# Moving layer 2's first layer norm: 14 token tiles normalised and split in layer 1's spatial stage, ten of them stored and turned on loading

## The chip, the cores and the metric

One core of one Trainium2 chip runs the whole program as one launch. The metric is the device time of a launch in microseconds (us). The engines are named as in the profile: PE (TensorE, matmul), DVE (VectorE), ACT (ScalarE), POOL (GpSimd), SP (SyncE, which here issues the DMAs).

## The reference, cut to what matters

Two identical layers work on `x`, 2048 tokens by 640 features, float32. Each adds an attention with a compressive memory (32 heads of 20, four segments of 512 tokens), then a gMLP whose spatial product mixes all tokens:

```python
x = x + _A_ref(_layernorm(x, axis=-1), A_wq, A_wk, A_wv, A_wo, A_beta)
x = x + _B_ref(_layernorm(x, axis=-1), B_w_in, B_w_sp, B_b_sp, B_w_out)
x = x + _A_ref(_layernorm(x, axis=-1), A_wq, A_wk, A_wv, A_wo, A_beta)
x = x + _B_ref(_layernorm(x, axis=-1), B_w_in, B_w_sp, B_b_sp, B_w_out)
def _layernorm(x, axis=-1, eps=1e-5):
    m = jnp.mean(x, axis=axis, keepdims=True)
    v = jnp.var(x, axis=axis, keepdims=True)
    return (x - m) / jnp.sqrt(v + eps)
```

In `_B_ref` the spatial part is `g = einsum("ts,bsf->btf", w_sp, z2) + b_sp` and the output `einsum("bsf,fd->bsd", z1 * g, w_out)`. The change touches the third of these layer norms, the one ahead of layer 2's attention.

## The kernel before, in words

The tokens are cut into 16 tiles of 128; four tiles are one attention segment. Float32 values are carried through the matmuls as two float16 halves, high and low, and three products. A *split* makes these halves (ACT copies the high one, POOL or DVE subtracts for the low one), and a *turn* brings them from tokens-by-features into features-by-tokens with one transposing DMA issued by SP.

Each layer has three stages, which stand in the profiled execution at these times. Layer 1: attention (`phase1a`) to about 610 us, projections of the gMLP (`phase1b`) to 820, spatial stage (`phase2`) 820 to 1221. Layer 2: attention 1221 to 1760, `phase1b` to 1950, spatial stage (`phase2s`, another routine) to the end.

**Layer 1's spatial stage** goes over the 16 token tiles `t`. `product(t)` is the spatial matmul (L713). Behind it in program order stand the store of an earlier output tile, `split(t+1)` of the next weight rows, loads, `gate(t)` (ACT reads the product from PSUM at L724, DVE multiplies with `z1` at L726, and the result `u` is split and turned into `ut`), `scale(t+2)`, and `tail(t-1)`: the output matmul L745 and the addition L748, which makes the output tile `xo`. `xo` is stored to the DRAM tensor `x2_t`, layer 2's input. In iterations 6 to 9 this stage also runs `prep` of layer 2's tiles 0 to 3; in 10 to 13 it computes their values (`value`), and in 14 and 15 the first query and key units. There the orders of PE, SP, DVE and ACT are as written in the code (`manual_schedule`), POOL's is left to the scheduler.

**`prep(t)`** makes the attention input of token tile `t`: load `x2_t`; statistics on DVE (`bn_stats` twice L235, `bn_aggr` L236, `ve` L237); the power -1/2 on POOL (L238); the normalisation on DVE (L1074); split on ACT (L250) and POOL (L251); the turn (L252) into `self.xt[s % 2]`, the transposed input of segment `s = t // 4` (two buffers: `xt0` for even segments, `xt1` for odd). For tiles 4 to 15 `prep` is called in layer 2's attention.

**Attention** goes over pairs of heads. A pair's stack of queries, keys, masks and row maxima is a tile `qk`, filled by DMAs: `qk<-st` (L1272, from the DRAM tensor `st`, where `stack` stored the halves `qhl` and `khl` of a unit at L1261 and L1262) and `qk<-mr` (L1353, the row maxima). For each pair PE does the score products L1314 (`mp` for the maxima, which DVE reduces at L1330, then `es`, which ACT exponentiates into `P` at L1323) and the value products. Between the pairs PE runs denser work in the order of a list, which is for layer 2

```python
order = "02 03 v4 04 v5 v6 v7 10 11 12 13 14 v8 v9 v10 20 v11 21 p0 22 23 24 v12 v13 v14 30 v15 31 p1 32 33 p2 34 p3 ..."
```

with `20 v11 21` and `30 v15 31` changed to `v11 20 21` and `v15 30 31` and `33 p2` to `p2 33`. Two digits `sm` are unit `m` of segment `s` (its query and key projections, PSUM tiles `qps` and `kps`, L1152; `keys` then makes `phl` and turns it into `pk`, L1188), `vi` is the value projection of tile `i` (`vps`, L1095), and `pi` an output projection. `vi` reads the tile that `prep(i)` turned. In attention only PE's order is as written. A list scheduler sets the others: it takes instructions by priority on its own simulated clock, and `hold()` (`issue_after`) keeps `prep`'s instructions behind what was last issued when they were written. Each DMA of SP also waits for the one eight issues before it.

Of the kernel before, what the change touches and what calls it, by code (L numbers as in the profile page):

```python
# [9 lines left out]
F32 = mybir.dt.float32  # L10
F32R = mybir.dt.float32r
F16 = mybir.dt.float16
# [3 lines left out]
ALU = mybir.AluOpType  # L16
# [3 lines left out]
S, D, H, DH, NSEG = 2048, 640, 32, 20, 4  # L20
# [7 lines left out]
XS = 1024.0  # L28
# [197 lines left out]
def layernorm_stats(g, xt, d, nch, mult=1.0):  # L226

    nc = g.nc
    st = g.small.tile([128, nch, 6], F32, tag="lnst", name="lnst")
    mv = g.small.tile([128, 2], F32, tag="lnmv", name="lnmv")  # L230
    ve = g.small.tile([128, 1], F32, tag="lnve", name="lnve")
    rs = g.small.tile([128, 1], F32, tag="lnrs", name="lnrs")
    c = d // nch
    for i in range(nch):
        nc.vector.bn_stats(st[:, i, :], xt[:, i * c:(i + 1) * c])  # L235
    nc.vector.bn_aggr(mv, st)  # L236
    nc.vector.tensor_scalar(ve, mv[:, 1:2], EPS, mult ** -2, ALU.add, ALU.mult)  # L237
    nc.gpsimd.tensor_tensor(rs, ve, g.mhalf, ALU.pow)  # L238
    return mv, rs


def layernorm(g, xt, out, d, nch, mult=1.0):
    mv, rs = layernorm_stats(g, xt, d, nch, mult)
    return g.nc.vector.tensor_scalar(out, xt, mv[:, 0:1], rs, ALU.subtract, ALU.mult)


def split_t(g, hl, t, src, low=None):

    nc = g.nc
    nc.scalar.copy(hl[:, 0], src)  # L250
    (low or nc.vector).tensor_tensor(hl[:, 1], src, hl[:, 0], ALU.subtract)  # L251
    nc.sync.dma_start(t.rearrange("p i k c -> p (i k) c"), hl.rearrange("p i c -> p (i c)"), transpose=True)  # L252
# [404 lines left out]
def phase2(g, w_sp, x1_d, z1_d, zh, zl, out, nxt):  # L657

    nc, tc = g.nc, g.tc
# [3 lines left out]
    with ExitStack() as ctx:  # L663
# [6 lines left out]
        py = pool("cy", 1, space=PSUM)  # L670
        nxt.pd = pool("cpd", 2, space=PSUM)
        small = lambda nm: g.small.tile([128, 1], F32, tag=nm, name=nm)
        raw, ready, un = {}, {}, {}

        def rows(t):
            if t < NT:
                raw[t] = pr.tile([128, S], F32, tag="wr", name="wr")
                nc.sync.dma_start(raw[t], w_sp[t * 128:(t + 1) * 128, :])

        def scale(t):  # L680
            if t < NT:
                am, iv, un[t] = small("am"), small("wiv"), small("un")
                pw, ivw = g.wpw[:, t:t + 1], g.wiv[:, t:t + 1]
                nc.vector.tensor_reduce(am, raw[t], AX.X, ALU.max, apply_absolute_value=True)
                nc.vector.tensor_scalar(pw.bitcast(I32), am.bitcast(I32), 0x7F800000, None, ALU.bitwise_and)
                nc.vector.tensor_scalar(pw, pw, 2.0 ** -100, None, ALU.max)
                nc.vector.reciprocal(iv, pw)
                nc.vector.tensor_scalar(ivw, iv, WB, None, ALU.mult)
                nc.vector.tensor_scalar(un[t], pw, 1.0 / (WB * ZS), None, ALU.mult)

        def split(t, i):
            if t < NT:
                if i == 0:
                    ready[t] = (pt0, pt1)[t % 2].tile([128, 2, 2, NT // 2, 128], F16, tag=f"wt{t % 2}", name="wt")
                v = raw[t].rearrange("p (m i c) -> p i m c", i=2, c=128)[:, i]
                ivw = g.wiv[:, t:t + 1]
                p = i and t > 0
                hl = (ph1 if p else ph0).tile([128, 2, 1024], F16, tag=f"wn{int(p)}", name="wn")
                h, l = [hl[:, j].rearrange("p (m c) -> p m c", c=128) for j in range(2)]
                nc.scalar.activation(h, v, AF.Identity, scale=ivw)  # L700
                nc.vector.scalar_tensor_tensor(l, v, ivw, h, ALU.mult, ALU.subtract)
                nc.sync.dma_start(ready[t][:, i].rearrange("p l k c -> p (l k) c"), hl.rearrange("p l c -> p (l c)"), transpose=True)

        def store(t):
            for i in range(t % 2, 2):
                nc.sync.dma_start(g.turned[t][i], ready[t][:, i].rearrange("p l k c -> p (l k c)"))

        def product(t):
            gp = pg.tile([128, 2, 512], F32, tag="gp", name="gp")
            for i, k in enumerate(ks):  # L710
                for j, (a, b) in enumerate(((0, zh), (0, zl), (1, zh))):
                    for n in range(2):
                        nc.tensor.matmul(gp[:, n, :FHH], ready[t][:, k % 2, a, k // 2, :], b[:, k, n * FHH:(n + 1) * FHH],  # L713
                                         start=(i == 0 and j == 0), stop=(i == NT - 1 and j == 2))
            return gp

        def fetch(nm, src):
            o = p2.tile([128, src.shape[-1]], F32, tag=nm, name="c" + nm)
            nc.sync.dma_start(o, src)
            return o  # L720
# [19 lines left out]
        def tail(t, uh, ul, xs, x1):  # L740
            yp = py.tile([128, 2, 512], F32, tag="yp", name="cyp")
            for k in range(KO):
                for j, (a, b) in enumerate(((uh, woh), (uh, wol), (ul, woh))):
                    for n in range(2):
                        nc.tensor.matmul(yp[:, n, :320], a[:kn[k], k, :], b[:kn[k], k, n * 320:(n + 1) * 320],  # L745
                                         start=(k == 0 and j == 0), stop=(k == KO - 1 and j == 2))
            xo = px.tile([128, 2, 320], F32, tag="xo", name="xo")
            nc.vector.scalar_tensor_tensor(xo, yp[:, :, :320], xs, x1.rearrange("p (n c) -> p n c", n=2), ALU.mult, ALU.add)  # L748
            return lambda: nc.sync.dma_start(out[t], xo.rearrange("p n c -> p (n c)"))

        def behind(k):
            held = ExitStack()
# [22 lines left out]
        for t in range(NT):  # L775
            gp = product(t)
            sent()
            split(t + 1, 0)
            split(t + 1, 1)
            z1 = fetch("z1", z1_d[t])  # L780
            rows(t + 2)
            if t == 0:
                run(g.wu.load(sp, D, "wu", False))
            x1 = fetch("x1", x1_d[t])
            store(t)
            if t == 4:
                g.wu.keep()
            if 6 <= t < 10:
                parts = nxt.prep(t - 6)
            now = *gate(t, gp, z1), x1  # L790
            scale(t + 2)
            if 6 <= t < 10:
                for f in parts:
                    f()
            if pend is not None:
                sent = tail(*pend)
            pend = now
            if 10 <= t < 14:
                run(nxt.value(t - 10))
            if t >= 14:  # L800
                run(nxt.unit(0, t - 14))
        sent()
        tail(*pend)()


# [94 lines left out]
class Attention:  # L900
# [9 lines left out]
    def __init__(self, g, x, o_d, x1_d, kept):  # L910
        self.g, self.nc, self.tc = g, g.nc, g.tc
        self.x, self.o_d, self.x1_d = x, o_d, x1_d
        self.st = g.st
        self.u1, self.u2, self.vs, self.xt, self.mst = kept
        self.xt, self.vs = [self.xt, None], [self.vs, None]
        self.gm, self.ot = {}, {}
        self.phq = {}
        self.P, self.Pf, self.mx = {}, {}, {}
        self.pv, self.o = {}, {}
        self.wait, self.last, self.stacked = [], -1, -1  # L920
        self.held, self.readout = {}, set()
        self.now, self.later, self.rd = None, {}, set()
        self.last_of, self.marks = {}, {}

    def post(self, k, f, free=False):

# [53 lines left out]
    def head(self):  # L980
# [3 lines left out]
        with ExitStack() as ctx:  # L984
# [69 lines left out]
            for t in range(4):  # L1054
                for _ in self.value(t):
                    pass
                if t == 0:
                    with self.hold():
                        self.start()

    def prep(self, t, lead=False):

        g, nc = self.g, self.nc
        s, c = t // 4, slice((t % 4) * 128, (t % 4) * 128 + 128)
        xt = self.e2.tile([128, D], F32, tag="xt", name="xt")
        nc.sync.dma_start(xt, self.x[t])
        ln = []

        def stats():
            ln.extend(layernorm_stats(g, xt, D, 2, XS))  # L1070

        def norm():
            mv, rs = ln
            nc.vector.tensor_scalar(xt, xt, mv[:, 0:1], rs, ALU.subtract, ALU.mult)  # L1074
            hl = self.e1.tile([128, 2, D], F16, tag="xh", name="xnhl")
            split_t(g, hl, self.xt[s % 2][:, :, :, c], xt, low=nc.gpsimd)

        def held(f):
            with self.tc.high_priority(offset=HP) if lead else self.hold():
                f()  # L1080

        return lambda: held(stats), lambda: held(norm)
# [567 lines left out]
```

## Time and profile before

| | |
|---|---|
| runs | 2294.73, 2294.86, 2304.04 us (median 2294.86) |
| profiled execution | 2289.98 us, its span 2288.3 us |
| busy, share of the span | PE 94 %, DVE 66 %, ACT 51 %, POOL 43 % |
| mean granted TensorE clock | 0.987 |
| DMA | 350.41 MB, mean 153 GB/s |

The profiled execution lies 4.88 us below the median of the runs; 1.7 us of it lie outside the span. Rows give a line of the code (L1074), engine, operation, output`<-`input, and times in us (single instructions in ns where the row says "mean"). "Idle" is time in which an engine stood still ahead of an instruction, with what released it behind `<-`. PEclk is the granted TensorE clock as a share of the full one.

### The profile page before, as it was taken

To read this page: it belongs to the slowest core of one execution; us is meant where nothing else is said; L and a number is where in the kernel's file an instruction comes from. 1 tells how busy PE (TensorE), PEld (TensorE's weight loads), DVE (VectorE), ACT (ScalarE), POOL (GpSimd) and SP (SyncE) were. 2 spreads that over 40 slices of the span, in tenths; PEclk is the share of its full clock that TensorE was granted. 3 is DMA by queue.
4 is the path that set the end of the run, shared out by engine and by line. 5 is a ranking of instruction groups with operands and counts; after the bars stand their busy time and mean duration, and the time that the engine had idled before them with its cause. 6 is when DMAs were issued, how large, how long until landed. Compare 5 with 4: busy or idle time off the path is not lost.

```text
span 2288.3 us, 50426 instructions
## 1 busy us (share of the span) xinstructions
PE 2141.0 (94%) x20487; PEld 1285.7 (56%) x20487; DVE 1503.9 (66%) x2812; ACT 1174.3 (51%) x1464; POOL 975.1 (43%) x728
## 2 busy tenths in 40 slices
PE   4888899999799999999998888999998999999999
PEld 2555565656555555555554555656665555555655
DVE  7688878788755545354335788797776767556454
ACT  3389788788632332112112888887875334322221
POOL 2188788888610100000001889888885323000000
PEclk9999999999999999999999999999999999999999
DMA  5544634456655677878645336353466433977875
GB/s 161 154 109 122 156 84 125 117 146 144 170 133 141 176 199 198 253 196 215 177 122 140 77 109 165 96 124 103 123 170 174 110 104 100 264 215 188 227 211 128
DMA packets 512008, 350.41 MB, mean 153 GB/s; under 512 B 409952, under 2 KB 447712, under 8 KB 506656
## 3 DMA queue, kind: packets, MB, share of 16 engines
q1 hardware_dynamic: 511776, 347.19, 57.7%
q8 instruction: 160, 2.62, 0.5%
q14 instruction: 72, 0.59, 0.1%
HBM read 161.10 MB, written 97.93 MB: 113 GB/s over the span
## 4 chain that ended last, share of the span: by engine, by line
PE 69%; DVE 11%; ACT 7%; DMA 4%; issue 4%; POOL 4%; SPq 0%; ACTq 0%; DVEq 0%; POOLq 0%
PE zp L334 15%; PE gp L713 12%; PE cyp L745 4%; PE cyp L548 3%; PE pv L1367 3%; DVE mx L1330 3%; PE ga L499 3%; PE gb L499 3%; PE yps L1128 3%; PE vps L1095 3%; PE qps L1152 3%; ACT PH L1340 3%; PE mp L1314 2%; PE kps L1152 2%; POOL PL L1341 2%
## 5 line engine op out<-in xcount | busy, mean ns | idle before, releaser
L1341 POOL TENSOR_TENSOR PL<-P,PH 128x1280 f16<-128x1280 f32 x248 | 649.9, 2623 | 140.4 <-ACT PH L1340 135.8
L1330 DVE TENSOR_REDUCE mx<-mp 128x2 f32<-128x1024 f32 (+3 forms) x512 | 408.2, 818 | 93.9 <-PE mp L1286 92.5
L1323 ACT ACTIVATE P<-es,sc 128x1024 f32<-128x1024 f32 (+1 forms) x384 | 370.2, 964 | 118.2 <-PE es L1286 111.5
L1340 ACT CAST PH<-P 128x1280 f16<-128x1280 f32 x256 | 320.5, 1253 | 23.0 <-PE pv L1367 13.7
L238 POOL TENSOR_TENSOR lnrs<-lnve,mhalf 128x1 f32<-128x1 f32 x92 | 57.4, 632 | 579.6 <-DVE lnve L237 578.5
L334 PEld LDWEIGHTS <-th 128*128 128x128 f16 x1920 | 187.6, 98 | 164.6 <-DMA th<-xnhl 1.9
L713 PE MATMUL gp<-zh,wt 128*128 128x432 f16 x1024 | 231.2, 346 | 0.0
L713 PEld LDWEIGHTS <-wt 128*128 128x128 f16 x1536 | 150.2, 98 | 128.9
L1314 PEld LDWEIGHTS <-qk 60*128 60x128 f16 (+1 forms) x2048 | 93.5, 94 | 226.6 <-issue 167.3
L499 PEld LDWEIGHTS <-wt 128*128 128x128 f16 x1344 | 131.5, 98 | 112.6
L1314 PE MATMUL es<-qk 64*128 64x512 f16 (+3 forms) x1024 | 135.6, 300 | 44.5 <-ACT P L1323 35.5
L1367 PE MATMUL pv<-vs,PH 128*128 128x41 f16 x2560 | 168.6, 182 | 1.7 <-DVE ab L1383 1.4
L1367 PE MATMUL pv<-vs,PL 128*128 128x41 f16 x2560 | 163.8, 181 | 6.5 <-POOL PL L1341 6.0
L1314 PE MATMUL mp<-qk 60*128 60x512 f16 (+3 forms) x1024 | 138.2, 307 | 32.7 <-DVE mx L1330 31.7
L1095 PE MATMUL vps<-wvh,xt 128*128 128x320 f16 x640 | 151.9, 303 | 8.8 <-DVE vs L1101 6.6
L1367 PEld LDWEIGHTS <-PH 128*128 128x128 f16 x2560 | 142.6, 96 | 13.7 <-ACT PH L1340 1.7
L334 PE MATMUL zp<-wi1h,th 128*128 128x432 f16 x640 | 148.2, 346 | 2.0 <-DVE x L1134 1.3
L1367 PEld LDWEIGHTS <-PL 128*128 128x128 f16 x2560 | 142.8, 96 | 8.3 <-POOL PL L1341 7.3
L713 PE MATMUL gp<-zl,wt 128*128 128x432 f16 x512 | 135.3, 346 | 0.0
L1152 PE MATMUL kps<-xt,wkh 128*128 128x512 f16 x380 | 121.8, 388 | 8.7 <-DVE lnve L237 5.7
L726 DVE TENSOR_TENSOR u<-u,cz 128x864 f32<-128x864 f32 x16 | 17.0, 1060 | 165.7 <-ACT u L724 123.3
L1128 PE MATMUL yps<-woh,o 128*128 128x320 f16 x480 | 116.6, 306 | 1.4 <-DVE x L1134 1.4
(261 smaller groups left out, 4391.7 us busy)
## 6 DMA issues: line engine op xcount, KB each, us to landing
wr<-in_B_w_sp_dram SPq DMA_DIRECT2D x32, 1024.0 KB
qk<-st SPq DMA_DIRECT2D x256, 120.0 KB
x<-x SPq DMA_DIRECT2D x56, 320.0 KB
z<-z SPq DMA_DIRECT2D x32, 432.0 KB
cz<-z SPq DMA_DIRECT2D x32, 432.0 KB
turned<-wt SPq DMA_DIRECT2D x24, 512.0 KB
wt<-turned SPq DMA_DIRECT2D x24, 512.0 KB
st<-qhl SPq DMA_DIRECT2D x40, 256.0 KB
```

Of the source, the lines that this page charges most:

```text
L334: nc.tensor.matmul(zp[:, n, :FHH], a[:, k, :], b[:, k, c:c + FHH], start=(k == 0 and j == 0), stop=(k == KD - 1 and j == 2))
L499: nc.tensor.matmul(o[:, :FHH], wt[:, x, m, :], zb[b][:, y, m, :], start=start and i == j == 0, stop=i == NP - 1 and j == 2, skip_group_che ...
L713: nc.tensor.matmul(gp[:, n, :FHH], ready[t][:, k % 2, a, k // 2, :], b[:, k, n * FHH:(n + 1) * FHH], start=(i == 0 and j == 0), stop=(i == ...
L1095: nc.tensor.matmul(ps, a[:, k, c], b[:, k, n * 320:(n + 1) * 320], start=(i == 0), stop=(i == 14))
L1128: nc.tensor.matmul(ps, a[:, k, :], b[:, k, c], start=(i == 0), stop=(i == 14))
L1152: nc.tensor.matmul(ps, a[:, k, c], b[:, k, :], start=(i == 0), stop=(i == 14))
L1314: nc.tensor.matmul(out[:, h, o:o + w], a[r, ac], b[r, bc], start=o == 0, stop=False, skip_group_check=True)
L1323: self.last_of["ACT"] = nc.scalar.activation(P[:, :, 512 * c:512 * c + ew], es[:, :, :ew], AF.Exp, scale=g.esc).ins
L1330: self.last_of["DVE"] = nc.vector.tensor_reduce(self.mx[m][:, :, i], mp[:, :, o:o + w], AX.X, ALU.max).ins
L1340: nc.scalar.copy(PH, P[:, h])
L1341: (nc.gpsimd if h == 0 or n < self.N - self.TAIL else nc.vector).tensor_tensor(PL, P[:, h], PH, ALU.subtract)
L1367: nc.tensor.matmul(pv[:, i, h, :], x[:, c:c + 128], v[:, j, h0 + h, :], start=(j == 0 and x is PH), stop=(j == i and x is PL), skip_group_ ...
```

## The change

A new method `early(t, x)` does the normalisation and the split of layer 2's tile `t` from layer 1's output tile `xo`, which is still in SBUF, so that no load is needed. Iterations 2 to 15 of layer 1's spatial stage call it for tiles 0 to 13, ahead of `gate(t)`. Tiles 0 to 3 are turned at once into `xt[0]`, as before. For tiles 4 to 13 the two halves are stored as they are (320 KB) to a DRAM tensor `xn{t}`, and `prep(t)` in layer 2's attention becomes one transposing DMA from there (L1080). Tiles 14 and 15 keep the old `prep`. The `prep` calls of iterations 6 to 9 go.

```diff
@@ phase2
-        raw, ready, un = {}, {}, {}
+        raw, ready, un, made = {}, {}, {}, {}
...
             xo = px.tile([128, 2, 320], F32, tag="xo", name="xo")
+            made[t] = xo.rearrange("p n c -> p (n c)")
             nc.vector.scalar_tensor_tensor(xo, yp[:, :, :320], xs, x1.rearrange("p (n c) -> p n c", n=2), ALU.mult, ALU.add)
-            return lambda: nc.sync.dma_start(out[t], xo.rearrange("p n c -> p (n c)"))
+            return lambda: nc.sync.dma_start(out[t], made[t])
...
-            if 6 <= t < 10:
-                parts = nxt.prep(t - 6)
+            if t > 1:
+                nxt.early(t - 2, made.pop(t - 2))
             now = *gate(t, gp, z1), x1
             scale(t + 2)
-            if 6 <= t < 10:
-                for f in parts:
-                    f()
@@ Attention
+    def early(self, t, x):
+        g, nc = self.g, self.nc
+        xt = self.e2.tile([128, D], F32, tag="xt", name="xt")
+        layernorm(g, x, xt, D, 2, XS)
+        hl = self.e1.tile([128, 2, D], F16, tag="xh", name="xnhl")
+        if t < 4:
+            split_t(g, hl, self.xt[0][:, :, :, t * 128:(t + 1) * 128], xt, low=nc.gpsimd)
+            return
+        nc.scalar.copy(hl[:, 0], xt)
+        nc.gpsimd.tensor_tensor(hl[:, 1], xt, hl[:, 0], ALU.subtract)
+        self.normed[t] = nc.dram_tensor(f"xn{t}", (128, 2, D), F16, kind="Internal").ap()
+        nc.sync.dma_start(self.normed[t], hl)

     def prep(self, t, lead=False):
...
+        if t in self.normed:
+            o = self.xt[s % 2][:, :, :, c]
+            return lambda: None, lambda: nc.sync.dma_start(o.rearrange("p i k c -> p (i k) c"), self.normed[t].rearrange("p i c -> p (i c)"), transpose=True)
```

Line numbers of the kernel after are up to 16 higher than before from here on (L1152 becomes L1168, L1272 becomes L1288). The normalisation of the moved tiles stands at L244, in `layernorm`.

DVE, in an iteration of layer 1's spatial stage: `wn` is the low half of weight rows, `u` the gated product, `vs` values of an earlier tile. Before:

```order
L748 SCALAR_TENSOR_TENSOR xo<-cyp,xs,cx_15284 128x640
L1101 SCALAR_TENSOR_TENSOR vs<-vps,vs 128x16x20 x2
L701 SCALAR_TENSOR_TENSOR wn<-wr,wiv,wn 128x1024 x2
L726 TENSOR_TENSOR u<-u,cz_15723 128x864
L728 TENSOR_REDUCE uam<-u 128x1
```

The same place in the kernel after:

```order
L749 SCALAR_TENSOR_TENSOR xo<-cyp,xs,cx_15355 128x640
L1117 SCALAR_TENSOR_TENSOR vs<-vps,vs 128x16x20 x2
L701 SCALAR_TENSOR_TENSOR wn<-wr,wiv,wn 128x1024 x2
L235 BN_STATS lnst<-xo 128x6 x2
L236 BN_AGGR lnmv<-lnst 128x2
L237 TENSOR_SCALAR lnve<-lnmv 128x1
L244 TENSOR_SCALAR xt<-xo,lnmv,lnrs 128x640
L726 TENSOR_TENSOR u<-u,cz_15824 128x864
L728 TENSOR_REDUCE uam<-u 128x1
```

Five instructions of the norm now stand ahead of the gate's multiplication; 14 iterations have them.

SP, where layer 2's attention begins: `xnhl` are a tile's two halves, `x2_14` and `x2_15` layer 1's last output tiles. Before:

```order
L749 DMA x2_14<-xo_16226 128x640
L1272 DMA qk4_16389<-st0 60x1024
L1272 DMA qk5_16396<-st0 60x1024 x2
L252 DMA_TRANSPOSE xt1_16392<-xnhl_16466 128x10x128
L749 DMA x2_15<-xo_16323 128x640
L1261 DMA st0<-qhl_16475 128x512
L1262 DMA st0<-qhl_16475 128x2x512
L1066 DMA xt_16564<-x2_6 128x640
L1261 DMA st0<-khl_16502 128x512
L252 DMA_TRANSPOSE xt1_16392<-xnhl_16471 128x10x128
L1262 DMA st0<-khl_16502 128x2x512
```

After:

```order
L750 DMA x2_14<-xo_16372 128x640
L1288 DMA qk4_16535<-st0 60x1024
L1288 DMA qk5_16542<-st0 60x1024 x2
L750 DMA x2_15<-xo_16469 128x640
L1080 DMA_TRANSPOSE xt1_16538<-xn4 128x10x128
L1080 DMA_TRANSPOSE xt1_16538<-xn5 128x10x128
L1277 DMA st0<-qhl_16591 128x512
L1278 DMA st0<-qhl_16591 128x2x512
L1277 DMA st0<-khl_16618 128x512
L1278 DMA st0<-khl_16618 128x2x512
L1080 DMA_TRANSPOSE xt1_16538<-xn6 128x10x128
L1080 DMA_TRANSPOSE xt1_16538<-xn7 128x10x128
```

Two turns instead of one stand ahead of the store of `qhl`, and the turns of tiles 6 and 7 directly behind that of `khl`.

SP some 30 us later, among the fetches of the first pairs (`pk` are turned keys, `mr` row maxima). Before:

```order
L1188 DMA_TRANSPOSE pk_16608<-phl_16605 128x8x128
L1261 DMA st0<-khl_16760 128x512
L1353 DMA qk1_16386<-mr_16771 2x4x128
L1262 DMA st0<-khl_16760 128x2x512
L1353 DMA qk1_16386<-mr_16771 2x4x128
L1066 DMA xt_16828<-x2_7 128x640
L1272 DMA qk0_16385<-st0 60x1024 x2
L1188 DMA_TRANSPOSE pk_16817<-phl_16814 128x8x128
L1353 DMA qk2_16387<-mr_16890 2x4x128 x2
```

After:

```order
L1204 DMA_TRANSPOSE pk_16722<-phl_16719 128x8x128
L1080 DMA_TRANSPOSE xt0_174<-xn8 128x10x128
L1277 DMA st0<-khl_16861 128x512
L1080 DMA_TRANSPOSE xt0_174<-xn9 128x10x128
L1278 DMA st0<-khl_16861 128x2x512
L1369 DMA qk1_16532<-mr_16872 2x4x128 x2
L1080 DMA_TRANSPOSE xt0_174<-xn10 128x10x128
L1288 DMA qk0_16531<-st0 60x1024
L1204 DMA_TRANSPOSE pk_16918<-phl_16915 128x8x128
L1288 DMA qk0_16531<-st0 60x1024
L1080 DMA_TRANSPOSE xt0_174<-xn11 128x10x128
L1369 DMA qk2_16533<-mr_16989 2x4x128 x2
```

The turns of tiles 8 to 11, which segment 2 reads, now stand here, long before their values; their buffer `xt0` is free once unit 04 has been computed. The turns of tiles 12 and 13 stand behind unit 14 (about 1400 us in the execution before).

More of the change, by code (lines that the diff above doesn't have):

```diff
@@ L923, in __init__ @@
         self.last_of, self.marks = {}, {}
+        self.normed = {}
     def post(self, k, f, free=False):
```

## The prediction

> **What bounds the kernel now.** I read the page first, then busy time in stretches of layer 1's spatial stage and layer 2's attention, then what PE waits for in that attention, then groups and the timeline at the waits that the change touches. The page:
>
> ```profile
> span 2288.3 us, 50426 instructions
> PE 2141.0 (94%) x20487; PEld 1285.7 (56%) x20487; DVE 1503.9 (66%) x2812; ACT 1174.3 (51%) x1464; POOL 975.1 (43%) x728
> PE 69%; DVE 11%; ACT 7%; DMA 4%; issue 4%; POOL 4%; SPq 0%; ACTq 0%; DVEq 0%; POOLq 0%
> ```
>
> PE is the bound: busy 94 %, and 69 % of the chain that ended last. The change leaves PE's work and its order as they are, so it can only win idle time of PE, 147.3 us in all, or clock.
>
> Busy time by stretch (columns after the length: busy us and instructions of each engine, granted clock, DMA share, GB/s):
>
> ```profile
> core 0: us, PE busy (x) PEld busy (x) DVE busy (x) ACT busy (x) POOL busy (x), PEclk, DMA share, GB/s
> 820.00:1221.00 401.00, 401.00 (x2389) 233.41 (x2388) 177.90 (x311) 84.62 (x93) 13.82 (x17) 1.00 0.72 193
> 1221.00:1760.00 539.00, 491.54 (x6884) 311.44 (x6883) 410.13 (x801) 413.55 (x521) 429.60 (x291) 0.98 0.48 125
> 1221.00:1241.00 20.00, 14.25 (x65) 5.76 (x64) 7.92 (x14) 5.75 (x9) 5.42 (x5) 0.84 0.70 170
> 1261.00:1281.00 20.00, 16.16 (x249) 11.36 (x243) 15.94 (x31) 15.40 (x19) 12.68 (x7) 1.00 0.30 75
> 1371.00:1431.00 60.00, 53.31 (x777) 35.56 (x778) 51.21 (x107) 48.72 (x64) 54.60 (x40) 1.00 0.59 160
> 1431.00:1501.00 70.00, 67.78 (x983) 42.92 (x980) 55.21 (x109) 58.27 (x75) 60.24 (x42) 1.00 0.33 90
> 1501.00:1541.00 40.00, 36.73 (x490) 22.61 (x487) 37.37 (x74) 31.88 (x42) 33.83 (x26) 0.91 0.56 145
> 1541.00:1571.00 30.00, 26.22 (x385) 18.61 (x382) 21.65 (x45) 22.54 (x31) 27.61 (x22) 0.97 0.48 101
> ```
>
> Layer 1's spatial stage, which receives the norms, is PE without a gap, with DVE busy 44 %, ACT 21 % and POOL 3 %. Layer 2's attention, which loses them, leaves PE idle for 47.5 us while DVE, ACT and POOL are each busy for over 75 %. So the work goes from where the other engines are short to where they have room. The stretches with the norms of tiles 4 and 5 (1221 to 1241), 7 (1261 to 1281), 8 to 11 (1371 to 1431) and 12 and 13 (1501 to 1541) have PE idle for 29, 19, 11 and 8 %; the stretch 1431 to 1501, which has no norm, for 3.2 %. The excess over 3.2 % is 3.2 us in the second, 4.8 in the third and 2.0 in the fourth. That is the pool of the gain; 1541 to 1571 (tiles 14 and 15) has an excess of 2.8.
>
> **What the change removes from the attention.** By form, 1221 to 1760:
>
> ```profile
> L251 POOL TENSOR_TENSOR xnhl<-xt,xnhl 128x640 f16<-128x640 f32 x12 | 17.2, 1434 | 10.0 <-ACT xnhl L250 8.5 <-PE es L1286 1.4
> L1074 DVE TENSOR_SCALAR xt<-xt,lnmv,lnrs 128x640 f32<-128x640 f32 x10 | 14.7, 1471 | 0.0
> ...
> L235 DVE BATCH_NORM_STATS2 lnst<-xt 128x6 f32<-128x320 f32 x20 | 8.8, 482 | 0.6 <-DMA xt<-x 0.5
> L250 ACT CAST xnhl<-xt 128x640 f16<-128x640 f32 x12 | 8.6, 720 | 12.3 <-DMA xt<-xnhl 6.2 <-PE cyp L745 3.1 <-DVE xt L1074 1.7
> L238 POOL TENSOR_TENSOR lnrs<-lnve,mhalf 128x1 f32<-128x1 f32 x12 | 6.6, 551 | 7.8 <-DVE lnve L237 7.8
> ```
>
> For ten tiles (tiles 4 and 5 were already normalised, in part, before 1221): POOL 10 x (1.43 + 0.55) = 20 us, DVE about 8 x (2 x 0.48 + 1.47) = 19 us, ACT 10 x 0.72 = 7 us, and ten loads of 320 KB; the ten turns stay. None of this is on PE, so it counts only where PE waits.
>
> **What it adds in layer 1's spatial stage: nothing.** Groups of 820 to 1221:
>
> ```profile
> L724 ACT ACTIVATE u<-gp,bsp,un 128x864 f32<-128x864 f32 x16 | 17.1, 1069 | 161.7 <-PE gp L713 161.7
> ...
> L1074 DVE TENSOR_SCALAR xt<-xt,lnmv,lnrs 128x640 f32<-128x640 f32 x6 | 3.7, 613 | 3.4 <-POOL lnrs L238 3.3
> ```
>
> The new rows stand ahead of the gate. Per tile DVE gets 2 x 0.48 of statistics, some 0.3 for two small rows, 0.57 of waiting for POOL's power (3.4 / 6) and 0.61 of normalisation: 2.5 us. ACT gets 0.72, POOL 0.55 + 1.43. ACT stands still for 161.7 / 16 = 10.1 us per tile until PE ends the product, and the new work fits in that time, since `xo` is made an iteration earlier. On SP the new store waits for POOL's subtraction, and what queues behind it is the gate's turn `ut`, which comes later still. Ten stores of 320 KB (0.33 MB) less four loads are 2 MB on the 77 MB of the stage (193 GB/s for 401 us), 2.5 % on a DMA share of 0.72. If the cover were gone, 14 x 2.5 = 35 us would be on the path. Ends 0 (PE has no gap there to win) and a loss of 35; I take 0, since a delay must exceed 10 us to reach PE.
>
> **Start of the attention, 1221 to 1241 (tiles 4 and 5).** Timeline (start, duration), then two rows of the chain for the landing times:
>
> ```profile
> 1224.75 0.89 DVE L748 SCALAR_TENSOR_TENSOR xo<-cyp,xs,cx 128x640 f32<-128x640 f32 x1 [5.79 <-DMA x<-xo]
> ...
> 1225.70 1.36 SPq L252 DMA_TRANSPOSE xt<-xnhl  x1
> ...
> 1227.10 0.70 SPq L749 DMA_DIRECT2D x<-xo  x1
> 1227.91 0.38 SPq L1261 DMA_DIRECT2D st<-qhl  x1
> 1228.38 0.41 SPq L1262 DMA_DIRECT2D st<-qhl  x1
> ...
> 1229.15 0.72 ACT L250 CAST xnhl<-xt 128x640 f16<-128x640 f32 x1 [5.52 <-DMA xt<-xnhl]
> ...
> 1233.90 0.69 ACT L1185 ACTIVATE phl<-kps,sc 128x512 f16<-128x512 f32 x1 [2.94 <-DVE kps L1176]
> ...
> 1234.97 0.70 DVE L1186 SCALAR_TENSOR_TENSOR phl<-kps,sc,phl 128x512 f16<-128x512 f32 x1
> ...
> 1235.72 1.01 PE L1152 MATMUL kps<-xt,wkh 128*128 128x512 f16 x2 [5.66 <-DVE lnve L237]
> ```
>
> ```profile
> 1215.97 2.16 DMA st<-khl
> ...
> 1225.70 3.38 DMA xt<-xnhl
> ```
>
> PE waits 5.66 us for the PSUM tile that `phl` reads last; the row names `lnve`, but `phl` (L1186) ends at 1235.67. ACT's copy for tile 5 waited 5.52 us for a turn and held up everything behind it on ACT. That goes. What is late next is the halves' buffer: `phl` takes the one of `qhl`, so `qhl` must have been stored. By the order SP now issues `x2_15` (ready at 1225.6), two turns and then `qhl`: 1225.7 + 0.70 + 2 x 1.36 + 0.79 and two gaps of some 0.08 is 1230.1. With a landing of 2.16 to 3.38 and 0.69 + 0.70 for `phl`, PE goes on between 1233.7 and 1234.9: a gain of 0.8 to 2.0. I take 1.5. Upper end: the whole wait, and with it the halved clock behind it (7 x (1 - 0.53) = 3.3, next rows), 9.0. Lower end: two turns instead of one ahead of `qhl`, nothing else won: -1.4.
>
> **The ramp, 1261 to 1281 (tile 7; turns of 8 to 11 now amid the fetches).** Tile 7's normalisation leaves DVE (1.47). Two turns now stand ahead of the `qk<-mr` of a pair; at 1.36 each, half of it on the path is 1.4. I take 0. Ends: the whole excess, +3.2, and four turns' issue in full on the path, -5.4.
>
> **1371 to 1431 (tiles 8 to 11).** A row of ACT's timeline, and two of the tile views for the turn from DRAM (`o`, median, mean and longest ns) beside those from SBUF:
>
> ```profile
> 1417.19 0.59 ACT L1394 CAST ohl<-oat 128x480 f16<-128x480 f32 x1 [2.00 <-DMA xt<-xnhl]
> ```
>
> ```profile
> L1110 SPq DMA_TRANSPOSE o<-o x24: 1327/1372/2324, 330.9 to 1742.9; - x24
> ```
>
> ACT's output split waits 2.00 us behind a copy that needs the buffer of a turn. Copies, subtractions and turns of these four tiles leave the stretch; the turns have long landed. Excess 4.8 us, less half a turn (0.7) for those of tiles 12 and 13, which now stand near it on SP: 4.1. Ends: the two turns in full on the path and nothing won, -2.7, and 4.8. A turn from DRAM costs SP 1.37 us, as from SBUF, so I count no more for it.
>
> **1501 to 1541 (tiles 12 and 13).** The clock by stretches of PE, and the two waits of PE's timeline ahead of the slow part:
>
> ```profile
> core 0: us, PE busy (x), PEclk, DMA share, GB/s
> 1528.00:1536.00 8.00, 7.02 (x64) 0.57 0.49 145
> 1235.00:1242.00 7.00, 6.28 (x22) 0.53 0.32 86
> ```
>
> ```profile
> 1526.05 0.28 PE L1314 MATMUL es<-qk 64*128 64x256 f16 x2 [0.61 <-ACT P L1323]
> ...
> 1528.98 0.61 PE L1314 MATMUL mp<-qk 60*128 60x512 f16 x2 [1.55 <-DVE mx L1330]
> ```
>
> DVE's normalisation stands ahead of the maxima for which PE waits, and after these two waits, 2.2 us in 3.5, the granted clock is 0.57 over 8 us: 3.4 us of lost work. With the norms gone I expect the waits to go (the excess, 2.0) and the drop with them, since they stand right ahead of it: 5.4. Ends 0 (nothing is added there) and 5.4.
>
> [...]
>
> **1541 to 1571 (tiles 14 and 15 keep `prep`):** 0, since their work is unchanged. Ends 0 and 2.8, its excess.
>
> **Sum:** 1.5 + 0 + 4.1 + 5.4 = 11.0 us. Against the profiled execution (span 2288.3, 2289.98 with what lies around it) that is 2279.0; it ran 4.9 us under the median of 2294.86, from which I get 2283.9. A change of 0.5 %, 11.5 us, is about what a measurement can tell from none.
>
> **Rivals.** (1) The start clears too. If ACT's copy was the true cause and `qhl` is stored in time, the wait of 5.66 and its clock drop go (9.0 in place of 1.5), and a lighter POOL queue takes the excess of tiles 14 and 15 (2.8): 21.3 us, 2273.6. For it: ACT's 5.52 us. Against: two turns now ahead of `qhl`.
> What PE waits for most at the scores in the attention (us in all, times, longest):
>
> ```profile
> PE es L1314 <- ACT P L1323: 13.2, 20, 1.4
> PE mp L1314 <- DVE mx L1330: 9.9, 17, 1.5
> PE es L1314 <- DMA qk<-mr: 7.7, 4, 4.1
> ```
>
> (2) The waits refill. These are short and on ACT, DVE and DMA in turn, so that the next dependency may close a gap, and a drop of the clock may come at another place. Only the start and half of 1371 to 1431 stay: 1.5 + 2.0 = 3.5 us, 2291.4. That DVE is busy for 51 of 60 us there speaks for it.
> (3) Slower: the turns in the way. Eight turns of 320 KB (tiles 4 to 11) now stand at the start and in the ramp among `st` and `mr` transfers. PE's longest wait for an `mr` transfer was 4.1. If each holds the chain for its landing time, 3.38 us, 8 x 3.38 = 27.0 us are lost and 11.0 won: 2310.9. It decides from 11.0 + 11.5 = 22.5 us, 2.8 per turn. Against it: SP's own part is 1.36, the DMA share there is 0.30, and PE has other work between the pairs.
> (4) The drop stays. If the clock near 1528 falls for another cause than the two waits ahead of it, its 3.4 us are not won: 11.0 - 3.4 = 7.6, 2287.3. For it: waits of over 1 us stand at other places without a drop, since PEclk is 1.00 in 1371 to 1431, where PE is idle for 11 %. Against it: the two here are close together. [...]
>
> **How the numbers follow.** Forecast (a gain of 8 to 17 us, 2278 to 2287): 0.44. Rival 1: 0.17. Rival 2: 0.19. Rival 3: 0.08. Rival 4: 0.10. The late gate in the spatial stage: 0.02, at 2330. Faster by over 0.5 %: rival 1 and that part of the forecast with a gain over 11.5, 0.28, together 0.45. Slower: most of rival 3 and the late gate, 0.09. Same: the rest, 0.46. The range leaves out rival 3, the late gate (0.10) and the part of rival 1 under 2270 (0.05); its upper end lies 5.6 us over rival 2, about the lower end of the ramp's term: 2270 to 2297.
>
> **What would show it.** Right: only two sets of L235 to L238 (tiles 14 and 15) in the attention, PE idle under 3 us in 1371 to 1431, clock near 1.00 at 1528, the first wait for `kps` about 4 us and still with a clock of half behind it, layer 1's spatial stage still at 401 us with PE full. Wrong: longer `qk<-mr` waits of PE or a spread between score products from 1255 to 1285 (rival 3); `es` and `mp` waiting as long as before, 23 us over the attention, with other names (rival 2); PE gaps at L745 in the spatial stage (late gate).

## The result, and the profile after

The changed kernel took 2274.74 us (median of 4, 2271.51 to 2278.71) against 2294.80 before: ratio 0.992, 95 % interval 0.9896 to 0.9944. Run a second time on another occasion ("again" below) it gave 0.993 (0.9915 to 0.9946). So it is faster by 0.7 to 0.8 %, 17 to 20 us. The profiled execution took 2271.51 us. Its page, and its stretches of the spatial stage, of the attention and of the places that the prediction named:

```profile
span 2269.1 us, 50425 instructions
PE 2135.3 (94%) x20487; PEld 1282.5 (57%) x20487; DVE 1501.6 (66%) x2812; ACT 1175.6 (52%) x1464; POOL 976.3 (43%) x728
```

```profile
core 0: us, PE busy (x) PEld busy (x) DVE busy (x) ACT busy (x) POOL busy (x), PEclk, DMA share, GB/s
817.00:1218.00 401.00, 401.00 (x2389) 233.46 (x2388) 191.76 (x351) 92.33 (x104) 32.04 (x35) 1.00 0.74 197
1218.00:1740.00 522.00, 484.98 (x6881) 308.89 (x6880) 394.32 (x761) 406.89 (x511) 412.52 (x273) 0.99 0.49 123
1218.00:1238.00 20.00, 15.84 (x81) 7.10 (x80) 7.98 (x11) 4.90 (x8) 0.69 (x1) 0.91 0.80 187
1363.70:1418.60 54.90, 52.71 (x776) 35.22 (x778) 43.53 (x85) 45.73 (x60) 46.56 (x32) 1.00 0.54 132
1488.50:1523.20 34.70, 33.69 (x491) 21.41 (x487) 32.17 (x64) 31.20 (x41) 30.08 (x22) 1.00 0.51 138
1523.00:1555.00 32.00, 28.91 (x419) 20.53 (x416) 24.12 (x49) 23.37 (x31) 28.00 (x22) 0.95 0.39 90
```

The spatial stage still takes 401 us with PE full, although DVE, ACT and POOL have 14, 8 and 18 us more to do there. The attention is 17 us shorter, and PE's idle time in it falls from 47.5 to 37.0 us. What PE waits for there:

```profile
PE es L1330 <- ACT P L1339: 10.0, 14, 1.4
PE mp L1330 <- DVE mx L1346: 8.2, 17, 2.8
PE es L1330 <- DMA qk<-mr: 7.2, 4, 4.0
PE kps L1168 <- DVE phl L1202: 4.2, 2, 3.8
```

PE runs the same matmuls in the same order in all kernels of this study. So a stretch can be measured from one of its instructions to another, wherever it lies in time. The table gives lengths of such stretches (us). The row "before" and the last column give the lengths themselves, all other fields the difference to the profile before. The stretches are named by their times in that profile. B is the sum of 1248 to 1276 and 1276 to 1290; the columns left out (1290 to 1371, 1431 to 1501, 1576 to 1661) change by 0.31 or less.

| kernel | A 1221-1248 | B 1248-1290 | C 1371-1431 | D 1501-1541 | E 1541-1576 | 1661-1760 | attention |
|---|---|---|---|---|---|---|---|
| before | 26.96 | 42.22 | 59.70 | 39.99 | 35.00 | 99.12 | 539.07 |
| after | -2.78 | -1.60 | -4.82 | -5.31 | -1.09 | -1.02 | 522.46 |
| again | -4.25 | -1.61 | -4.80 | -5.30 | -1.02 | +0.94 | 523.08 |
| keep1213 | -2.76 | -1.47 | -4.98 | +0.78 | -1.31 | +0.05 | 529.38 |
| keep811 | -2.41 | -1.63 | +2.96 | -5.31 | +0.11 | +2.31 | 535.10 |
| keep47 | +0.43 | -0.17 | -4.68 | -5.31 | -2.27 | +1.29 | 528.42 |
| stores | +0.19 | -0.33 | +0.80 | +2.42 | +0.03 | +0.28 | 542.79 |
| dveback | +0.36 | -0.23 | -0.85 | -4.42 | -2.36 | +0.98 | 532.65 |
| splitback | -2.92 | -0.22 | -4.32 | -4.52 | -2.14 | +0.60 | 525.81 |
| jit | -2.10 | -1.63 | -4.49 | -5.32 | -0.95 | +0.82 | 525.53 |
| behind | -2.52 | -1.65 | -4.82 | -5.32 | -0.99 | -1.19 | 522.65 |
| spread47 | -6.17 | -0.21 | -4.82 | -5.30 | -1.10 | +0.84 | 522.51 |
| all16 | -1.94 | +0.58 | -0.07 | -5.30 | -5.41 | -1.11 | 525.94 |
| chain1213 | -2.52 | -1.55 | -4.84 | -1.90 | -0.82 | -1.60 | 525.75 |

Of the gain of 16.6 us (16.0 in "again"), A, B, C and D make 14.5 (16.0) and E 1.1 (1.0). The last 1.0 stands in 1661 to 1760; in "again" that stretch is 0.9 longer than before, so this is no steady gain. Beyond the attention the times of single executions spread without the change: PE's work up to 610 us, at which none of the edits is aimed, took 603.4 us in this execution and 606.6 in that of before, and 603.4 to 615.0 over all 14.

### The profile page after: what moved, and what is told of

It reads as the page before. It is cut to its first block, busy times and chain, and to the rows that moved or that the text cites. A ratio compares the mean times of both kernels' runs of the same rounds, so it can differ in the third digit from the quotient of the medians.

```text
span 2269.1 us, 50425 instructions
## 1 busy us (share of the span) xinstructions
PE 2135.3 (94%) x20487; PEld 1282.5 (57%) x20487; DVE 1501.6 (66%) x2812; ACT 1175.6 (52%) x1464; POOL 976.3 (43%) x728
## 5 line engine op out<-in xcount | busy, mean ns | idle before, releaser
L1168 PE MATMUL kps<-xt,wkh 128*128 128x512 f16 x380 | 120.7, 385 | 6.3 <-DVE phl L1202 6.3
L1168 PE MATMUL qps<-xt,wqh 128*128 128x512 f16 x380 | 116.9, 379 | 1.6 <-DMA xt<-xnhl 1.2
```

The costliest lines, as they stand in the source:

```text
L1168: nc.tensor.matmul(ps, a[:, k, c], b[:, k, :], start=(i == 0), stop=(i == 14))
```

## The experiments

**Which tiles pay where.** Three kernels leave one group of tiles with the old `prep`.

```diff
-            if t > 1:
+            if t > 1 and t - 2 < 12:                 # keep1213
+            if t > 1 and not 8 <= t - 2 < 12:        # keep811
+            if t > 1 and not 4 <= t - 2 < 8:         # keep47
                 nxt.early(t - 2, made.pop(t - 2))
```

> Tiles 12 and 13 keep the old preparation in layer 2's attention; tiles 0 to 11 are moved as in the kernel after. The attention (PE's work from 1221 to 1760 in the profile before) took 539.1 us before and 522.5 after. Local theory (each stretch's gain belongs to the norms that stood in it): PE's work of 1501 to 1541 loses its 5.3 us again, clock drop included, all other stretches stay as after within 0.5 us, attention 527.8 us. Rival, spread theory (less load on all engines and a new order from the scheduler win everywhere a little): two tenths of 16.6, 3.3 us, not bound to that stretch, attention 525.8 us.

Measured: 2287.02 us, ratio 0.9959 (0.9944 to 0.9974). D is back at 40.77, all other stretches up to E stay within 0.3 us of after.

> Tiles 8 to 11 keep the old preparation; all else as in the kernel after. Local theory: PE's work of 1371 to 1431 loses its 4.8 us again, the other stretches stay within 0.5 us, attention 527.3 us. Spread theory: four tenths of 16.6, 6.6 us over several stretches, attention 529.1 us. If the four early turns of tiles 8 to 11 had cost anything in 1248 to 1290, that stretch would get faster than after, by up to 5 us.

Measured: 2285.59 us, ratio 0.9950 (0.9935 to 0.9965). C is back, and 3 us beyond before; A, B and D stay. B did not get faster without the four early turns. Of the 12.6 us that the attention lost, 7.8 are C; 1.2 are E and 3.3 are 1661 to 1760, where the clock is halved for 3.4 and 6.8 us longer than in the kernel after.

> Tiles 4 to 7 keep the old preparation; all else as in the kernel after. Local theory: PE's work of 1221 to 1290 loses its 4.4 us again (2.8 at the start, 1.6 in the ramp), later stretches stay within 0.5 us, attention 526.9 us. Spread theory: 6.6 us over the whole attention, 529.1 us.

Measured: 2282.98 us, ratio 0.9942 (0.9925 to 0.9958). A and B are back, C and D stay; E is 1.2 shorter than after, without its drop of the clock (3.4 us). Most of each loss lies where its tiles' norms stood, and the spread theory falls. Sizes are less regular: the three losses (6.9, 12.6 and 6.0) sum to 25.5, more than the 16.6 won. C of keep811 and D of keep1213 each hold a clock drop of 3.4 us:

```profile
1366.90:1429.50 62.60, 54.80 (x776) 36.03 (x778) 51.25 (x105) 48.42 (x64) 54.57 (x40) 0.97 0.63 163
```

```profile
1496.40:1537.10 40.70, 35.76 (x488) 22.40 (x484) 37.95 (x75) 31.70 (x42) 35.12 (x26) 0.96 0.56 149
```

**What the added part costs.** Early norms and stores stay, but the attention prepares tiles 4 to 15 as before.

```diff
-        if t in self.normed:
+        if t in ():
```

> Everything that the change adds in layer 1's spatial stage is kept (14 early norms, ten stores), but tiles 4 to 15 are prepared in the attention as before, so the ten stored tiles are not used. Local theory: the additions cost nothing, so spatial stage 401 us, attention 539 us, time as before, 2294.8 within 4 us. Rival (the additions cost something that the gain hid): slower than before by that cost; 14 tiles at 2.5 us would be 35 us.

Measured: 2297.56 us, ratio 1.0007 (0.9996 to 1.0018). Its spatial stage:

```profile
822.10:1223.10 401.00, 401.00 (x2389) 233.49 (x2388) 194.90 (x361) 92.38 (x103) 33.35 (x37) 1.00 0.74 198
```

So the 14 early norms cost nothing where they stand. In the kernel after, ACT still waits 115.4 us for PE's products there (161.7 before):

```profile
L724 ACT ACTIVATE u<-gp,bsp,un 128x864 f32<-128x864 f32 x16 | 17.1, 1070 | 115.4 <-PE gp L713 115.4
```

The attention of "stores" took 3.7 us more than before, 2.4 of it in D; why stays open.

**Which part of the preparation was the cost.** dveback brings back the load and DVE's part (with POOL's power), splitback the load, ACT's copy and POOL's subtraction, chain1213 all of it in its chain for tiles 12 and 13; each into a tile that nothing reads, with the turn still from DRAM.

```diff
         if t in self.normed:
+            xt = self.e2.tile([128, D], F32, tag="xt", name="xt")
+            nc.sync.dma_start(xt, self.x[t])
...
+                ln.extend(layernorm_stats(g, xt, D, 2, XS))                              # dveback, chain1213
+                nc.vector.tensor_scalar(xt, xt, mv[:, 0:1], rs, ALU.subtract, ALU.mult)  # dveback, chain1213
+                nc.scalar.copy(hl[:, 0], xt)                                             # splitback, chain1213
+                nc.gpsimd.tensor_tensor(hl[:, 1], xt, hl[:, 0], ALU.subtract)            # splitback, chain1213
```

> As the kernel after, but in layer 2's attention tiles 4 to 13 also get their load, the statistics, the power and the normalisation back, on DVE and POOL, into a tile that nothing reads; the copy, the subtraction and the turn from SBUF stay out. DVE theory (the normalisation ahead of the maxima is what PE waited for): 1501 to 1541 loses its 5.3 us again and 1371 to 1431 at least half of its 4.8. Split theory (ACT's copy, which waited for the landing of the turn before, held up ACT): all stretches as after within 1 us, attention 522.5 us.

> As the kernel after, but tiles 4 to 13 get their load, ACT's copy and POOL's subtraction back in the attention, into a tile that nothing reads, so that no copy waits for the landing of a turn; no statistics and no normalisation. DVE theory: all stretches as after within 1 us, attention 522.5 us. If the copies and subtractions as such were the cost: 1371 to 1431 loses 4.8 us again. If ACT's wait for the landing was the cost, this kernel shows none of it and dveback neither, and the sum of both stays well under 16.6 us.

Measured: dveback 2287.84 us, ratio 0.9961 (0.9947 to 0.9975); splitback 2282.84, 0.9945 (0.9924 to 0.9966). In A and C it is mostly DVE's part: dveback gives back 3.1 and 4.0 us, splitback 0 and 0.5. Of the 4.0, PE's longer work in a drop of the clock (PEclk 0.97 over 58.8 us) is 1.4, and before had no drop in C; so about 1.7 of C's 4.8 us are in neither kernel. PE's main wait in dveback's C:

```profile
PE mp L1344 <- DVE mx L1360: 3.4, 4, 1.8
```

In B each gives back 1.4 of 1.6, by different waits: dveback brings PE's wait for the maxima back (2.7 us before, 1.2 after, 2.4 in dveback), splitback has longer ones for ACT's `P`, for POOL and for `mr`. In D neither is enough: each gives back 0.8 to 0.9 of the 6.1 that keep1213 lost. Both theories fall there.

> As the kernel after, but tiles 12 and 13 get load, statistics, power, normalisation, copy and subtraction back in the attention, in a chain, into a tile that nothing reads; their turn still comes from DRAM. It asks why 1501 to 1541 kept its gain in dveback and in splitback, while keep1213 lost it (40.8 us against 34.7). Chain theory (the copy waits for the normalisation and holds up ACT's exponentials and DVE's maxima behind it): the stretch is back at 39 us or more. Buffer theory (tile 13's copy waited for the landing of tile 12's turn from SBUF): it stays at 36 us or less.

Measured: 2282.37 us, ratio 0.9942 (0.9921 to 0.9963). D is 38.1 us, between the two forecasts:

```profile
1497.70:1535.80 38.10, 34.72 (x490) 21.77 (x487) 35.55 (x73) 32.25 (x43) 33.59 (x26) 1.00 0.54 143
```

The chain gives back 3.4 us; keep1213 lost 2.7 more. Of that, 1.0 is PE's longer busy time (35.76 against 34.72), in a clock drop (PEclk 0.96 over 40.7 us) that this execution does not have. Whether the last 1.6 us, more idleness of PE, is the turn from SBUF stays open.

**Where the turns stand.**

```diff
+                with ExitStack() if lead else self.hold():                                  # jit
+                with self.tc.issue_after(self.put) if lead and t < 6 else ExitStack():      # behind
                     nc.sync.dma_start(o..., self.normed[t]..., transpose=True)
...
+        self.put = nc.sync.dma_start(rows[:, i:i + 2], hl).ins                              # behind, in stack()
...
-                    for d, f in zip((3, 5) if t > 0 else (1, 2), self.prep(i, t < 0)):
+                    for d, f in zip((3, 5) if t > 0 else (1, 3 if i < 6 else 2), self.prep(i, t < 0)):   # behind
```

> As the kernel after, but the turns of tiles 6 to 13 stand on SP behind the last fetch issued when they were written, as the old preparation did, and no longer at the start of the attention; nothing else changes. If the early place of the turns is free, as I hold: every stretch as after within 0.5 us, time as after, 2275 to 2280 us. Rival 3 of the prediction in small (the early turns cost in the ramp): 1248 to 1290 faster by 1 to 5 us. If the early landing was part of the gain: 1371 to 1431 slower by 1 to 5 us.

Measured: 2282.59 us, ratio 0.9922 (0.9891 to 0.9952). B, which now holds no such turn, is the same to 0.03 us, and C is 0.3 longer: the early place is free, and no part of the gain. The time lies above the forecast 2275 to 2280. The attention is 3.1 us longer than after's in this execution, 0.7 of it in A and 1.8 in 1661 to 1760; the two executions of one kernel, after and again, differ by 1.5 and 2.0 there.

> As the kernel after, but the turns of tiles 4 and 5 stand on SP behind the store of the first qhl of the attention and not ahead of it; nothing else moves. If the two turns are what holds phl's buffer at the start, PE's wait for kps of 3.8 us falls to about 1 and the clock stays near 1.00 there: PE's work of 1221 to 1248 is 3 to 5 us shorter than after. Rival: the values of tile 4 then wait for their turn, and the stretch stays as it is within 1 us.

Measured: 2278.72 us, ratio 0.9917 (0.9900 to 0.9934). A is no shorter. In the kernel after, the start looked as the prediction had it:

```profile
1217.74 0.38 PE L1168 MATMUL qps<-xt,wqh 128*128 128x512 f16 x1
...
1223.05 2.97 SPq L1080 DMA_TRANSPOSE xt<-xn  x2
...
1226.13 0.53 SPq L1277 DMA_DIRECT2D st<-qhl  x1
...
1229.28 0.69 ACT L1201 ACTIVATE phl<-kps,sc 128x512 f16<-128x512 f32 x1 [5.20 <-DMA st<-qhl]
1230.00 0.75 DVE L1202 SCALAR_TENSOR_TENSOR phl<-kps,sc,phl 128x512 f16<-128x512 f32 x1 [1.68 <-ACT phl L1201]
1230.81 0.59 PE L1168 MATMUL kps<-xt,wkh 128*128 128x512 f16 x2 [3.76 <-DVE phl L1202]
```

ACT's `phl` waits 5.20 us for the store of `qhl`, which SP issues behind two turns, and PE waits for `phl`. In "behind" PE waits 2.0 there, and 3.2 a little later:

```profile
PE vps L1116 <- DVE vs L1122: 3.2, 1, 3.2
PE kps L1173 <- DVE phl L1207: 2.0, 1, 2.0
```

The later wait has the same form. ACT's next `khl` waited for a store behind the turns of tiles 6 and 7, and the values (`vs`) that PE waits for stand behind `khl` on ACT:

```profile
1233.17 3.42 SPq L1083 DMA_TRANSPOSE xt<-xn  x2
...
1236.74 0.48 SPq L1282 DMA_DIRECT2D st<-qhl  x1
...
1237.47 0.37 SPq L1283 DMA_DIRECT2D st<-qhl  x1
...
1240.10 0.60 ACT L1186 ACTIVATE khl<-kps 128x512 f16<-128x512 f32 x1 [3.38 <-DMA st<-qhl]
```

So part of the wait moved to the next store. spread47 sets each of the four turns behind a store of its own:

```diff
+SLOT = {4: ("q", 0, 2), 5: ("q", 0, 3), 6: ("q", 0, 4)}   # in stack(): the turn behind this store; 7 behind the last one
```

> As the kernel after, but the turns of tiles 4 to 7 are spread: 4 behind the store of the first qhl (unit 02), 5 behind that of 03, 6 and 7 behind those of unit 04, so that no two stand together at the start. If the turns in a row hold the buffers that the stores must free (behind showed the wait move from kps, 3.8 to 2.0 us, to vps, 3.2 us), both waits fall under 1.5 us and PE's work of 1221 to 1248 is 2.5 to 4.5 us shorter than after. Rival (the start is bound by DVE and ACT, not by SP): the stretch stays within 1 us of after's 24.2.

> The kernel after once more, unchanged. In the traces so far the first 610 us of the program, which no kernel changes, took 603.3 to 615.0 us, while the attention of layer 2 repeats. I expect 522.5 us within 1.5 for the attention, and a time of 2272 to 2282 us that moves with the clock drops of the first 610 us.

Measured: spread47 2277.20 us, ratio 0.9920 (0.9905 to 0.9935); again 2279.45, 0.9930 (0.9915 to 0.9946). A is 1.9 shorter than in "again", 3.4 than in after; PE's wait for `vps` falls to the 1.1 us that it is in after, that for `kps` stays at 2.0 as in "behind" (forecast: both under 1.5). B gives 1.4 back, 1661 to 1760 is as long as in "again", and the attention is the same (522.51 against 522.46 and 523.08). So the wait at the start can be shortened, but nothing comes of it.

**The tiles that were left.** all16 adds tiles 14 and 15 to spread47, 14 by `early` in the last iteration, 15 by a norm and a store in the first pairs of the attention.

```diff
+            if t == 15:
+                nxt.early(14, made[14])
...
+            self.late(15)      # load at pair step -3, statistics at 2, norm, split and store at 5
```

> As spread47, and tiles 14 and 15 are stored too: 14 by an early norm in the last iteration of the spatial stage, 15 by a load, norm, split and store in the first pairs of the attention, where POOL is idle for 20 us; their prep becomes a turn. Local theory: the stretch 1541 to 1576, 33.9 us after, loses PE's wait of 2.8 us and the clock drop behind it (1.6), so 29.5 to 31.5; the ramp 1248 to 1290 pays at most 1 us; attention 516 to 518 us, time 2268 to 2275 us. Rival: tile 15's norm costs in the ramp what it costs later (2.5 us or more), and the attention stays at spread47's.

Measured: 2279.35 us, ratio 0.9933 (0.9916 to 0.9951), no better than after, and the attention is 525.94 us: both miss the forecast. E is 29.6 us as forecast, 4.3 less than after, with PE busy for 29.34 of 29.60. But A and B are 4.2 and 0.8 longer than in spread47, and C lost all that it had won. A holds two drops of the clock of 3.4 us, where spread47 has none (PEclk 1.00); what brought them stays open. The turns of tiles 12 to 15 now stand close together on SP, where unit 14 frees their buffer:

```profile
1407.58 1.56 SPq L1117 DMA_TRANSPOSE xt<-xn  x1
1409.23 2.15 SPq L1250 DMA_TRANSPOSE pk<-phl  x1
1411.43 1.36 SPq L1117 DMA_TRANSPOSE xt<-xn  x1
1412.89 1.14 SPq L1418 DMA_DIRECT2D qk<-mr  x2
```

```profile
1416.99 0.39 PE L1379 MATMUL es<-qk 64*128 64x512 f16 x2 [3.24 <-DMA qk<-mr]
```

The fetch of the maxima waits behind three turns (two of `xt`, one of `pk`), PE 3.24 us for it, and the clock is halved for 3.4 us behind that (PEclk of C 0.97), and PE's work in C takes 1.5 us longer than after. Together that is the loss of C, 4.75 us. A kernel that sets these two turns apart was not run.

## Why the prediction was right, and where its terms were off

**The cause was right, the sum too low.** PE's idle time by the norms of each group of tiles was the pool of the gain, and keep1213, keep811 and keep47 put each loss back in its place. The signs came: PE idle for 2.2 us in 1371 to 1431, a clock of 1.00 at the old drop, a first wait for `kps` of 3.8 us, and the spatial stage at 401 us. But 11.0 us were forecast, and the attention gave 16.6 and 16.0. The time of 2274.74 us lies in the range, but below the 2278 to 2287 that the forecast itself covered; that of "again", 2279.45, lies within.

**Spatial stage, 0 forecast:** 0.00 in the table's way of measuring (820 to 1221 took as long as before to 0.01 us), and "stores" shows it alone.

**Start, 1.5 forecast, 2.8 and 4.3 measured.** The step itself held: two turns ahead of `qhl`, `phl` late by its buffer. PE went on at 1230.81, which is 13.1 us after the stage began (1217.74); before it was 14.7, from

```profile
1221.06 0.38 PE L1152 MATMUL qps<-xt,wqh 128*128 128x512 f16 x1
```

to 1235.72: 1.6 us. What I left out is the clock behind it. I kept the drop in full; it lasted 6.8 us before, 3.4 after, and was absent in "again", and PE's busy time in A is 1.2 and 2.8 us shorter than before: that is the rest. What decides which of the two comes was not shown: PE's idle time in A is about 1.5 us shorter than before in both.

**Ramp, 0 forecast, 1.6 measured.** I set 1.5 for tile 7's normalisation against 1.4 for turns among the fetches. The first fits dveback, which loses 1.4 with the wait for the maxima. It is not shown alone, since splitback and spread47 lose the same 1.4 by other waits. The second cost nothing: in jit, without those turns, B is the same.

**1371 to 1431, 4.1 forecast, 4.8 measured.** For the turns of tiles 12 and 13 I took 0.7 off; PE waits only 0.2 us for `qk<-mr` there. The quoted wait of ACT for a turn was not the main cause: DVE's part gives back 4.0 by itself and copies alone 0.5. Whether ACT's wait, which neither kernel brings back, makes up what is missing was not tested.

**1501 to 1541, 5.4 forecast, 5.3 measured,** with the clock at 1.00 in its place.

**1541 to 1576, 0 forecast, 1.1 measured;** PE still waits for the norms of tiles 14 and 15, by other rows. Before, it waited 2.2 us for a turn and 1.1 for maxima; now it waits 3.1 for maxima, behind a normalisation:

```profile
1532.65 2.90 DVE L1090 TENSOR_SCALAR xt<-xt,lnmv,lnrs 128x640 f32<-128x640 f32 x1 [0.87 <-POOL lnrs L238]
```

all16 takes these waits out.

**The rivals.** Rival 1 gave a time close to the measured one, 2273.6, but not by its way: the start gained 3 to 4 us, not 9.0, and 1541 to 1576 1.1, not 2.8. That the number agrees is luck. Rival 2 falls by the table, and `es` and `mp` wait 18.2 us in place of 23.1. Rival 3 did not happen, and jit shows that there was no such cost; but all16 shows its mechanism where three turns stand in a row ahead of one fetch, for which PE waits 3.24 us. Its point of decision was misplaced: by these runs it is not the number of turns, but how many stand together ahead of a store or a fetch that PE needs. Rival 4 falls in D. The two rows for it are the last stretch at full clock before the drop, and the drop (length, PE busy, PEclk):

```profile
1524.90:1528.30 3.40, 1.92 (x36) 1.00 0.31 87
1528.30:1535.10 6.80, 6.12 (x57) 0.50 0.57 169
```

In 3.4 us PE stood still for 1.5, in parts of two waits (0.61 and 0.87), and the clock fell. I counted in all 14 traces how much idle time stood ahead of a drop. Drops last mostly 3.4, 6.8 or 10.2 us: in the clock records of before and after, of the 23 that end before the program does, 15 last 3.41 us, 7 last 6.83 and one 10.24, and each stretch at full clock is a whole multiple of 3.413 us (1 to 179 times, to 0.1 us). So I divided each stretch at full clock into pieces of 3.413 us and counted by PE's idle time in a piece (100 to 2250 us of each execution):

| idle in the piece, us | pieces | followed by half clock |
|---|---|---|
| under 0.9 | 8096 | 0 |
| 0.9 to 1.4 | 287 | 5 |
| 1.4 to 1.6 | 73 | 9 |
| 1.6 to 2.0 | 79 | 52 |
| over 2.0 | 82 | 82 |

So the clock fell behind none of the 8096 pieces with under 0.9 us of idleness, behind 52 of the 79 with 1.6 to 2.0, and behind all 82 with more. The count adds up all waits in a piece: 66 of the 148 drops counted here came after pieces with PE idle for under 2.0 us.

## What to carry to other kernels

Where one engine is the bound, compare its idle share in each stretch with that of a neighbouring stretch that lacks the work in question: the excess, with the clock lost behind it, was the gain to 0.1 us where several tiles' norms stood in the middle of the stage (4.8 and 5.4), and an upper bound in the ramp (3.2 for 1.6). At the start the whole wait with its drop, 9.0, was one too (for 2.8 and 4.3). Moving work into a stage where the bound engine has no gap was free here (401.00 us before and after), since the moved rows fit into the time in which the other engines waited for it (ACT 161.7 us before, 115.4 after). Transposing DMAs of 320 KB, each 1.4 us of the queue, cost nothing one by one among the fetches of the ramp (jit: B the same to 0.03 us). Two or three together stood ahead of a store or fetch that was then waited for by 3 us or more (5.20 and 3.38 behind two, 3.24 behind three), and 4.8 us were lost where the bound engine needed that fetch.

## What the runs showed of the hardware

That 52 of the 79 pieces of 3.4 us in which PE was idle for 1.6 to 2.0 were followed by a halved clock was not expected; small waits that fell together were dearer than their sum, since a drop of 3.4 us at a clock of 0.50 costs up to 1.7 more. The drops also fit why single executions of one kernel differ: A differed by 1.5 us between two profiles of the kernel after, with PE's idle time there the same to 0.2 us, one with a drop and one without. DVE's normalisation costs less in its new place, 0.613 us on average instead of 1.471:

```profile
L244 DVE TENSOR_SCALAR xt<-xo,lnmv,lnrs 128x640 f32<-128x640 f32 x14 | 8.6, 613 | 9.4 <-POOL lnrs L238 9.4
```

What makes it shorter was not shown. POOL is busy for 8 % of that stage (32.04 of 401.00 us), and for 80 % of the attention before (429.60 of 539.00).
